# The w_in product of a second MLP as seven block products instead of eight, in groups of 768 tokens

## The chip, the cores and the metric

One NeuronCore of a Trainium2 chip runs the kernel. The metric is the device time of one execution in microseconds (us). The engines are TensorE (PE, with PEld for its weight loads), VectorE (DVE), ScalarE (ACT), GpSimd (POOL) and SyncE (SP), which here issues all DMAs.

## The reference

4608 tokens (8 batches of 576), model width 512. A linear attention with an RMS norm makes x, a gated MLP (1536 wide) follows, and then the MLP that the change is about:

```python
def _moe2_ref(x, w_in, w_out) -> np.ndarray:      # x 4608x512, w_in 512x2048, w_out 2048x512
    h = x @ w_in
    beta = 1.0
    neg = h <= -beta
    pos = h >= beta
    g = np.where(pos, h, np.where(neg, 0.0, (h + beta) ** 2 / (4.0 * beta)))
    return (g @ w_out).astype(np.float32)
```

Inputs are float32 or float64 (the weights are float64 and are decoded to float32 on the chip). The products are made nearly exact: each operand is split in a high and a low half of type fp32r, and each product is the sum of three matmuls (high by high, high by low, low by high).

## The kernel before, in words

The tokens go in `NB` = 9 blocks of `T` = 512. The features of a hidden layer go in slices of `P` = 128, which the code counts by `f`.

The **first part** makes attention and the gated MLP of all nine blocks. For blocks 2 to 8 one pass of the loop over `f` (12 slices) issues 24 matmuls for gate and value of slice `f + 1` (`gate_value`), their activation, the splits of that slice and of its `w_out` rows (`split_g`, `split_wo`), a piece of the next block's attention (`late_piece`), and the 12 matmuls of `down(j, f)`. In six passes of a block `decode_w2` also turns one raw float64 slice of the second MLP's weights into float32 and writes it to DRAM (`w2d`). Finished blocks go to DRAM as `x2d`.

The **second part** is the loop over the nine blocks at the end. `hidden2(j, f)` makes one 128x512 slice of h: 4 chunks of the model width by 3 matmuls of 512 columns, weights stationary, tokens moving. `act2` makes g of it with one ScalarE and two VectorE instructions and splits g. `out2(j, f)` adds that slice's share of the output, 4 token chunks by 3 matmuls of 512 columns. The halves of w_in stay in SBUF for the whole part. Those of w_out don't: `split_wo` makes them again for each of the 9 x 16 slices.

```python
def mm3(ps, w, x, first, last, wsl=slice(None)):
    nc.tensor.matmul(ps, w[0][:, wsl], x[0], start=first, stop=False)
    nc.tensor.matmul(ps, w[0][:, wsl], x[1], start=False, stop=False)
    nc.tensor.matmul(ps, w[1][:, wsl], x[0], start=False, stop=last)
```

Each engine runs its instructions in the order of the program; the code is a schedule written out by hand. What an instruction needs from another engine it waits for at its place in its own engine's queue. A tile of a pool can be written again only when its former reader is done. DMAs are issued by SP in program order too, and an issue that waits holds those behind it.

Of the kernel before, what the change touches and what calls it, by code (L numbers as in the profile page):

```python
# [7 lines left out]
F32 = mybir.dt.float32  # L8
# [6 lines left out]
NT, DM, FF1, FF2 = B * S, H * D, 1536, 2048  # L15
P = 128
T = 512
NB = NT // T
NP = H // 2
KC = DM // P  # L20
TC = T // P
F1, F2 = FF1 // P, FF2 // P
NSC = S // P
SC = 112
SR = S - NSC * SC
# [4 lines left out]
@with_exitstack  # L30
def attn_gated_mlp_kernel(ctx: ExitStack, tc: tile.TileContext, a: dict, out: bass.AP):
    nc = tc.nc
    pool = lambda name, bufs, **kw: ctx.enter_context(tc.tile_pool(name=name, bufs=bufs, **kw))
    const = pool("const", 1)
    wp = pool("w", 60)
# [4 lines left out]
    h_p = pool("h", 1, space=bass.MemoryType.PSUM)  # L40
    at_p = pool("at", 2, space=bass.MemoryType.PSUM)
    dram = pool("dram", 1, space=bass.MemoryType.DRAM)

    wod = {f: dram.tile([P, T], F32, name=f"wod{f}") for f in range(4, 6)}
    w2d = [dram.tile([P, 2, T], F32, name=f"w2d{f}") for f in range(F2)]
# [12 lines left out]
    def act_copy(o, i):  # L58
        nc.scalar.activation(out=o, in_=i, func=AF.Copy)  # L59
# [247 lines left out]
    def decode(keys):  # L307
        outs = []
        run(decode_steps(keys, outs))
        return outs  # L310
# [33 lines left out]
    def decode_wo(*fs):  # L344

        aside = {4: "gl", 5: "gh"}

        def place(key):
            f = key[1]
            if f in aside:  # L350
                return gp.tile([P, T], F32, name="wof", tag=aside[f])
            return wp.tile([P, T], F32, name="wo", tag="w")

        ts = []
        yield from decode_steps([("wo", f) for f in fs], ts, place)
        for f, t in zip(fs, ts):
            if f in aside:
                nc.sync.dma_start(out=wod[f], in_=t)
            else:
                wo[f] = t  # L360

    def load_wo(f):
        wo[f] = wp.tile([P, T], F32, name="wo", tag="w")
        nc.sync.dma_start(out=wo[f], in_=wod[f])

    def decode_w2(f, i):
        t, = decode([("w2", f, i)])
        nc.sync.dma_start(out=w2d[f][:, i], in_=t)
# [35 lines left out]
    def new_acc():  # L404
        for c in range(4):
            acc[c] = acc_p.tile([P, T], F32, name=f"acc{c}", tag=f"acc{c}")
# [12 lines left out]
            nc.sync.dma_start(out=dst(c), in_=t)  # L419


    w2, wo2, g2 = {}, {}, {}

    def load_w2(f):
        w = temp("w2f", "dt", bufs=2)
        nc.sync.dma_start(out=w, in_=w2d[f][:, 0])
        wo2[f] = wp.tile([P, T], F32, name="wo2", tag="w")
        nc.sync.dma_start(out=wo2[f], in_=w2d[f][:, 1])
        w2[f] = split(w, half_tile(wp, "w", "w"), half_tile(wp, "w", "w"))

    def load_x2(j):
        for c in range(KC):
            xnext[c] = xp.tile([P, T], F32, name="xn", tag=f"xn{c}")
            nc.sync.dma_start(out=xnext[c], in_=x2d[j][:, c, :])

    def hidden2(j, f):
        h = h_p.tile([P, T], F32, name="h2", tag=f"h{f % 2}")
        for c in range(KC):
            mm3(h, w2[f], xs[c], c == 0, c == KC - 1, slice(c * P, (c + 1) * P))
        return h  # L440

    def act2(j, f, h):

        t = temp("t2", "sig")
        nc.scalar.activation(out=t, in_=h, func=AF.Relu, bias=half, scale=0.5)  # L445
        g = temp("g2", "gf")
        nc.vector.scalar_tensor_tensor(out=g, in0=t, scalar=1.0, in1=h, op0=ALU.min, op1=ALU.max)  # L447
        nc.vector.scalar_tensor_tensor(out=g, in0=t, scalar=1.0, in1=g, op0=ALU.min, op1=ALU.mult)  # L448
        n = (j * F2 + f) % 3
        if n < 2:  # L450
            hi, lo = half_tile(gp, "gh", "gh"), half_tile(gp, "gl", "gl")
        else:
            t = tp.tile([P, 2, T], F32R, name="g3", tag="raw", bufs=4)
            hi, lo = t[:, 0], t[:, 1]
        g2[j, f] = split(g, hi, lo)

    def out2(j, f):
        g, w = g2.pop((j, f)), wos.pop(f)
        if f == 0:
            new_acc()  # L460
        for c in range(TC):
            mm3(acc[c], g, w, f == 0, f == F2 - 1, slice(c * P, (c + 1) * P))

    def rows(j):
        return lambda c: out[j * T + c * P:j * T + (c + 1) * P, :]


    todo = [(f, i) for f in range(F2) for i in range(2)]
    with tc.manual_schedule():
        for p in range(NP):  # L470
            load_kv_early(0, p)
# [8 lines left out]
            load_kv_early(1, p)  # L480
            load_q(1, p, True)
        load_gv(1)
        xb = {p: wp.tile([P, T], F32, name="xb", tag="w") for p in range(NP)}
        xbt = [(half_tile(wp, "w", "w"), half_tile(wp, "w", "w")) for _ in range(KC)]
# [185 lines left out]
        for j in range(2, NB):  # L670
            more = j + 1 < NB
            for f in range(F1):
                if j + 2 < B and f in (0, 2, 4, 6):
                    load_kv(j + 2, f // 2)
                if f + 1 < F1:
                    g = gate_value(f + 1, xs)
                    split_g(j, f + 1, g)
                    split_wo(wo, f + 1)
                if more and f < 9:
# [3 lines left out]
                if not more and f == 8:  # L683
                    load_x2(0)
                down(j, f)
                if not more and f > 0:
                    load_w2(f - 1)
                if f == F1 - 2:
                    split_x()
                if f in (0, 2, 4, 6, 8, 9) and todo and ("w2", *todo[0]) in raws:  # L690
                    decode_w2(*todo.pop(0))
                if more and f in (1, 3, 5, 7, 8, 11) and todo:
                    load_raw(("w2", *todo[0]), a["w_2"][todo[0]])
                if f == F1 - 1:
                    store(lambda c: x2d[j][:, c, :])
                    if more:
                        split_wo(wo, 0)
                        split_g(j + 1, 0, gate_value(0, xs))
                        if j + 2 < NB:
                            load_q(j + 2, 0)  # L700
                            load_q(j + 2, 1)
        split_wo(wo2, 0)
        split_wo(wo2, 1)
        for f in range(3):
            act2(0, f, hidden2(0, f))
        for j in range(NB):
            more = j + 1 < NB
            for f in range(F2):
                out2(j, f)
                if f + 2 < F2 or more:  # L710
                    split_wo(wo2, (f + 2) % F2)
                if j == 0 and f + 11 < F2:
                    load_w2(f + 11)
                if f == 4 and more:
                    load_x2(j + 1)
                if f + 4 < F2:
                    act2(j, f + 3, hidden2(j, f + 3))
                elif f + 4 == F2:
                    h = hidden2(j, F2 - 1)
                    if more:  # L720
                        split_x()
                    act2(j, F2 - 1, h)
                elif f == F2 - 2 and more:
                    act2(j + 1, 0, hidden2(j + 1, 0))
            store(rows(j))
            if more:
                for f in range(1, 3):
                    act2(j + 1, f, hidden2(j + 1, f))


# [38 lines left out]
```

## Time and profile before

| | |
|---|---|
| median of 3 runs | 1808.94 us (1805.08 to 1809.77) |
| the profiled execution, its time | 1809.8 us |
| its span in the profile | 1808.0 us |
| PE busy | 1795.3 us (99%), 8272 matmuls |
| DVE busy | 1056.6 us (58%) |
| ACT busy | 753.1 us (42%) |
| granted TensorE clock, mean | 0.995 |

The time is that of the whole execution; the span goes from the first instruction to the last. Busy time of PE counts a matmul from its start to its modelled end, so neighbours overlap and the share says only that PE was never without work. How long a matmul holds the engine is read from the distance of two starts.

### The profile page before, as it was taken

How to read it: one execution, taken by the hardware profiler on the slowest of the kernel's cores; microseconds unless marked ns; L12 is line 12 of the kernel's file. 1: busy time of each engine (PE TensorE's matmuls, PEld its weight loads, DVE VectorE, ACT ScalarE, POOL GpSimd, SP SyncE). 2: the span in 40 equal slices, each digit the busy share in tenths (PEclk: the TensorE clock that was granted, in tenths of full speed). 3: DMA queues.
4: the chain of work that ended last, by engine and by line, in shares of the span. 5: the costliest groups of instructions: out<-in, count | busy, mean ns of one | idle time of the engine just before them, and what ended most of it. 6: DMA issues, size and time to landing. Idle time of an engine off the chain costs nothing.

```text
span 1808.0 us, 21195 instructions
## 1 busy us (share of the span) xinstructions
PE 1795.3 (99%) x8272; PEld 1454.9 (80%) x8272; DVE 1056.6 (58%) x1621; ACT 753.1 (42%) x1233; POOL 1.9 (0%) x9
## 2 busy tenths in 40 slices
PE   8999999999999999999999999999999999999999
PEld 5787778888888888887888888888888888888887
DVE  3788755767667575766533555454555555555554
ACT  4444444535454454544432434343333333333333
POOL 0000000000000000000000000000000000000000
PEclk9999999999999999999999999999999999999999
DMA  8454733132322322121022301010101010101000
GB/s 223 140 181 168 220 107 103 49 120 68 101 73 66 108 79 79 57 82 53 7 70 84 109 18 47 1 47 0 47 1 47 1 47 1 47 1 47 1 24 24
DMA packets 57365, 124.15 MB, mean 69 GB/s; under 512 B 6568, under 2 KB 10792, under 8 KB 57264
## 3 DMA queue, kind: packets, MB, share of 16 engines
q1 hardware_dynamic: 57264, 122.79, 21.6%
q8 instruction: 65, 1.06, 0.2%
q14 instruction: 36, 0.29, 0.1%
HBM read 88.69 MB, written 34.08 MB: 68 GB/s over the span
## 4 chain that ended last, share of the span: by engine, by line
PE 97%; DMA 1%; DVE 1%; issue 0%; ACT 0%; SPq 0%; DVEq 0%; ACTq 0%
PE h L78 18%; PE h L79 18%; PE h L80 18%; PE acc L78 13%; PE acc L80 13%; PE acc L79 12%; PE X L138 2%; PE kvps L117 1%; PE SSt L174 1%; DMA gload<-gd 1%; PE R L206 0%; DMA q_early<-in_qT 0%; PE SS L234 0%; PE SS L233 0%; PE rt L193 0%
## 5 line engine op out<-in xcount | busy, mean ns | idle before, releaser
L78 PE MATMUL h<-xh,w 128*128 128x512 f32 x1344 | 528.2, 393 | 0.0
L79 PE MATMUL h<-xl,w 128*128 128x512 f32 x1344 | 526.2, 392 | 0.0
L80 PE MATMUL h<-xh,w 128*128 128x512 f32 x1344 | 525.2, 391 | 0.2 <-DVE w L67 0.2
L78 PEld LDWEIGHTS h<-xh,w 128*128 128x128 f32 x1344 | 253.2, 188 | 56.7 <-ACT w L59 0.7
L80 PEld LDWEIGHTS h<-xh,w 128*128 128x128 f32 x1344 | 253.2, 188 | 55.6 <-DVE w L67 0.6
L79 PEld LDWEIGHTS h<-xl,w 128*128 128x128 f32 x1344 | 253.1, 188 | 54.0
L447 DVE SCALAR_TENSOR_TENSOR g<-t,h 128x512 f32<-128x512 f32 x144 | 98.9, 687 | 249.8 <-ACT t L445 248.7
L445 ACT ACTIVATE t<-h,half 128x512 f32<-128x512 f32 x144 | 98.9, 687 | 261.1 <-PE h L80 261.1
L391 DVE TENSOR_TENSOR gf<-sig,h 128x512 f32<-128x512 f32 x108 | 74.1, 686 | 186.1 <-PE h L80 104.7
L67 DVE TENSOR_TENSOR wol<-wo,woh 128x512 fp32r<-128x512 f32 x252 | 172.4, 685 | 15.4 <-ACT woh L59 15.4
L78 PE MATMUL acc<-gh,woh 128*128 128x512 f32 x432 | 177.1, 410 | 0.0
L80 PE MATMUL acc<-gh,wol 128*128 128x512 f32 x432 | 171.4, 397 | 0.2
L79 PE MATMUL acc<-gl,woh 128*128 128x512 f32 x432 | 171.1, 396 | 0.2 <-DVE gl L67 0.2
L59 ACT ACTIVATE woh<-wo 128x512 fp32r<-128x512 f32 x252 | 155.5, 617 | 14.5 <-PE acc L80 13.5
L78 PE MATMUL acc<-woh,gh 128*128 128x512 f32 x384 | 150.5, 392 | 0.0
L80 PE MATMUL acc<-woh,gl 128*128 128x512 f32 x384 | 150.2, 391 | 0.0
L79 PE MATMUL acc<-wol,gh 128*128 128x512 f32 x384 | 149.4, 389 | 0.0
L59 ACT ACTIVATE gh<-gf 128x512 fp32r<-128x512 f32 x84 | 53.1, 632 | 212.9 <-DVE gf L391 212.9
L59 ACT ACTIVATE gh<-g 128x512 fp32r<-128x512 f32 x96 | 60.7, 632 | 143.5 <-DVE g L448 143.5
L389 ACT ACTIVATE sig<-h 128x512 f32<-128x512 f32 x108 | 64.5, 597 | 115.1 <-PE h L80 109.5
L67 DVE TENSOR_TENSOR gl<-g,gh 128x512 fp32r<-128x512 f32 x96 | 66.5, 693 | 67.0 <-ACT gh L59 67.0
L448 DVE SCALAR_TENSOR_TENSOR g<-t,g 128x512 f32<-128x512 f32 x144 | 99.6, 692 | 5.0
(125 smaller groups left out, 2121.2 us busy)
## 6 DMA issues: line engine op xcount, KB each, us to landing
raw<-in_w SPq DMA_DIRECT2D x32, 512.0 KB, 3.8
raw<-in_w_gv SPq DMA_DIRECT2D x24, 512.0 KB, 4.4
kvraw<-in_kv_main SPq DMA_DIRECT2D x24, 448.0 KB, 5.4
x2d<-ev SPq DMA_DIRECT2D x36, 256.0 KB, 2.8
xn<-x2d SPq DMA_DIRECT2D x36, 256.0 KB, 4.8
out<-ev SPq DMA_DIRECT2D x36, 256.0 KB, 2.3
w2d<-dt SPq DMA_DIRECT2D x32, 256.0 KB, 2.4
qraw<-in_qT SPq DMA_DIRECT2D x28, 256.0 KB, 3.3
```

The source lines that it names most:

```text
L59: nc.scalar.activation(out=o, in_=i, func=AF.Copy)
L67: nc.vector.tensor_tensor(out=lo, in0=src, in1=hi.bitcast(F32), op=ALU.subtract)
L78: nc.tensor.matmul(ps, w[0][:, wsl], x[0], start=first, stop=False)
L79: nc.tensor.matmul(ps, w[0][:, wsl], x[1], start=False, stop=False)
L80: nc.tensor.matmul(ps, w[1][:, wsl], x[0], start=False, stop=last)
L117: nc.tensor.matmul(ps[s], kc[:, s], vc[:, s], start=c == 0, stop=c == NSC)
L138: nc.tensor.matmul(X[:, t0:t1], kvbd[b % NKV][:, p, :], q[:, t0:t1], start=True, stop=True)
L389: nc.scalar.activation(out=sig, in_=gate, func=AF.Sigmoid)
L391: nc.vector.tensor_tensor(out=g, in0=sig, in1=value, op=ALU.mult)
L445: nc.scalar.activation(out=t, in_=h, func=AF.Relu, bias=half, scale=0.5)
L447: nc.vector.scalar_tensor_tensor(out=g, in0=t, scalar=1.0, in1=h, op0=ALU.min, op1=ALU.max)
L448: nc.vector.scalar_tensor_tensor(out=g, in0=t, scalar=1.0, in1=g, op0=ALU.min, op1=ALU.mult)
```

## The change

The second part is rewritten as the class `Second`. Tokens go in 6 groups of 768, each as two halves of `T2` = 384. The w_in product is seen as a 2 x 2 by 2 x 2 product of blocks: two halves of the model width (256 each), two slices of features (`s` and `s + 8`), two halves of the tokens. It is made with seven block products (`product`) in place of eight, from sums of blocks of the weights (`s1` to `s4`) and of the tokens (`t1` to `t4`). A block product is 2 chunks by 3 matmuls of 384 columns. Partial results are taken from four PSUM banks (A, B, C, D), copied to SBUF by ScalarE (`saved`) and added by VectorE; banks A and B are accumulated on after they were copied. One step `s` of a group has 7 x 6 = 42 such matmuls, and 18 of 512 columns for the output (none in step 0, whose slices are due a step later). When the 8 steps of a group are over, 16 more output products follow, for the group's second token half.

The weights' sums and the halves of everything are made once, in the first part (`w2_steps`, six pieces after each `down`), and go to DRAM: `w2d` holds 14,336 bytes a partition for each of the 8 steps, `wo2d` 4096 for each of the 16 slices of w_out. `w_load` reads one step's 1.83 MB again in every group, into a pool of two buffers that it shares with the tokens of the next group (`x_load`). The w_out halves are read in the first group and stay.

The last block of the first part is split: the 12 slices of gate and value go first and are kept in DRAM (`gd`), then pools are closed, the first loads of the second part are issued, and the 12 `down` follow with the tokens' splits (`x_steps`) between them.

```diff
+    def w2_steps(unit):
+        kind, f = unit
...
+        if kind == "out":
+            yield from halves_out(outs[0], temp("hi", "du", bufs=2), lambda h: wo2d[f][:, h])
+            return
...
+        for o, x, y, op in ((s1, a21, a22, ALU.add), (s2, s1, a11, ALU.subtract), (s4, a12, s2, ALU.subtract), (s3, a11, a21, ALU.subtract)):
+            nc.vector.tensor_tensor(out=o, in0=x, in1=y, op=op)
+            yield
+        d = w2d[f]
+        yield from halves_out(a22, a21, lambda h: d[:, 2, h])
+        yield from halves_out(t0, t1, lambda h: d[:, 0:2, h])
+        yield from halves_out(u0, t0, lambda h: d[:, 3:5, h])
+        yield from halves_out(u1, u0, lambda h: d[:, 5:7, h])
...
-    def hidden2(j, f):
-        h = h_p.tile([P, T], F32, name="h2", tag=f"h{f % 2}")
-        for c in range(KC):
-            mm3(h, w2[f], xs[c], c == 0, c == KC - 1, slice(c * P, (c + 1) * P))
-        return h
...
+        def product(self, bank, w, x, first=True):
+            for c in range(2):
+                sl = slice(c * P, (c + 1) * P)
+                for n, (h, l) in enumerate(((0, 0), (0, 1), (1, 0))):
+                    nc.tensor.matmul(bank[:, :T2], self.ws[w][h][:, sl], self.xo[x][:, l, c], start=first and c == n == 0,
+                                     stop=c == 1 and n == 2, skip_group_check=True)
...
+            for s in range(HF):
+                A, D, B, C = (self.bank(n) for n in "ADBC")
+                self.ws = self.w_next
+                if s + 1 < HF:
+                    self.w_next = self.w_load(s + 1)
+                    if g == 0:
+                        self.wo2_load(s + 1)
+                        self.wo2_load(s + 1 + HF)
+                elif more:
+                    x = self.x_load(g + 1)
...
+                self.product(A, "a11", "b11")
+                s1 = self.saved(A, "p1")
...
+                self.product(D, "a12", "b21")
...
+                tt(c0[:, 0], D[:, :T2], s1, ALU.add)
+                self.product(B, "s1", "t1")
...
+                s5 = self.saved(B, "p5")
...
+                    self.out_product(acc, s - 1, this_hi, s == 1, False)
...
+                self.product(A, "s2", "t2", False)
+                u2 = self.saved(A, "u2")
...
+                self.product(C, "a22", "t4")
+                self.product(B, "s4", "b22", False)
+                tt(g1[s][:, 0], B[:, :T2], u2, ALU.add)
+                self.product(A, "s3", "t3", False)
+                u3 = self.saved(A, "u3")
+                tt(g1[s][:, 1], A[:, :T2], s5, ALU.add)
+                tt(c0[:, 1], C[:, :T2], u3, ALU.add)
+                if late is not None:
+                    self.out_product(acc, s - 1 + HF, late_hi, False, False)
...
+        for f in range(F1):
+            keep_g(0, f, gate_value(f, xs, tag="wol"))
+            run(work, 6)
+            if f >= F1 - 3:
+                load_g(0, f - F1 + 3)
...
+        split_g(last, 0, gf[0, 0])
+        split_wo(wo, 0)
+        load_g(0, 3)
+        second.begin()
+        for f in range(F1):
+            if f + 1 < F1:
+                split_g(last, f + 1, gf[0, f + 1])
+                split_wo(wo, f + 1)
+            if 0 < f < F1 - 3:
+                load_g(0, f + 3)
+            if f > 1:
+                run(second.xsteps, 1)
+            down(last, f)
```

What this puts in the queues is shown at three places. First TensorE in the second part; before, a slice of h (`h`, weights `w`, tokens `xh` and `xl`) follows on the output matmuls (`acc`) of another slice:

```order
L78 MATMUL acc_13597<-woh,gh 128x512
L79 MATMUL acc_13597<-wol,gh 128x512
L80 MATMUL acc_13597<-woh,gl 128x512
L78 MATMUL h_13915<-xh_13444,w 128x512
L79 MATMUL h_13915<-xl_13445,w 128x512
L80 MATMUL h_13915<-xh_13444,w 128x512
L78 MATMUL h_13915<-xh_13448,w 128x512
```

Now, step 0 of the first group and the begin of step 1 (`ch` are the four banks, `x_` the operands made of the tokens, `wst` one step's weights):

```order
L556 MATMUL chA_8578<-x_b11_8316,wst_8258 128x384 x6
L556 MATMUL chD_8579<-x_b21_8343,wst_8258 128x384 x6
L556 MATMUL chB_8580<-x_t1_8368,wst_8258 128x384 x6
L556 MATMUL chA_8578<-x_t2_8395,wst_8258 128x384 x6
L556 MATMUL chC_8581<-x_t4_8422,wst_8258 128x384 x6
L556 MATMUL chB_8580<-x_b22_8447,wst_8258 128x384 x6
L556 MATMUL chA_8578<-x_t3_8474,wst_8258 128x384 x6
L556 MATMUL chA_8651<-x_b11_8316,wst_8582 128x384 x6
L556 MATMUL chD_8652<-x_b21_8343,wst_8582 128x384 x6
L556 MATMUL chB_8653<-x_t1_8368,wst_8582 128x384 x6
L84 MATMUL acc2_0_8575<-wo2_0_8571,gh2_8617 128x512
```

The 12 matmuls of 512 columns of one slice became 42 of 384 columns for two slices of 768 tokens, and step 0 hands bank A straight to step 1, which reads other weights.

Second, SP's queue where the last block of the first part is split, which has no counterpart before (block 8's slices went from `gate_value` straight to `down`, and tokens and weights of the second part were read in pieces of 256 KB between the `down` of that block):

```order
L756 DMA gd0_11_121<-gf_8219 128x512
L454 DMA gload_8222<-gd0_2_112 128x512
L454 DMA gload_8249<-gd0_3_113 128x512
L517 DMA xin_8251<-x2d0_134 128x2x256 x2
L517 DMA xin_8251<-x2d1_135 128x2x256
L517 DMA xin_8251<-x2d0_134 128x2x256 x2
L517 DMA xin_8251<-x2d1_135 128x2x256
L505 DMA wst_8258<-w2d0_86 128x3584
L454 DMA gload_8292<-gd0_4_114 128x512
```

The load of slice 4 for `down` now stands behind the first group's tokens (six DMAs) and the first step's weights.

Third, SP's queue where one group ends and the next begins (`out` are the output's rows); before, nothing but the next block's tokens was read there:

```order
L505 DMA wst<-w2d_86 128x3584
L587 DMA out<-ev_11499 128x512
L587 DMA out<-ev_11502 128x512
L587 DMA out<-ev_11505 128x512
L587 DMA out<-ev_11702 128x512
L587 DMA out<-ev_11705 128x512
L587 DMA out<-ev_11708 128x512
L505 DMA wst<-w2d_87 128x3584
```

The weights of the next group's step 0 stand ahead of the group's last stores, those of its step 1 behind them.

## Rows read from the trace of the kernel before

**Rows 1.** The page, part 1 (busy time) and part 4 (chain that ended last)

```profile
PE 1795.3 (99%) x8272; PEld 1454.9 (80%) x8272; DVE 1056.6 (58%) x1621; ACT 753.1 (42%) x1233; POOL 1.9 (0%) x9
...
PE 97%; DMA 1%; DVE 1%; issue 0%; ACT 0%; SPq 0%; DVEq 0%; ACTq 0%
```

**Rows 2.** Windows: stretch, length, busy by engine (instructions), clock, DMA share, GB/s

```profile
300.00:400.00 100.00, 100.00 (x487) 81.36 (x485) 65.56 (x98) 47.68 (x76) 0.00 (x0) 1.00 0.27 82
...
1100.00:1800.00 700.00, 700.00 (x3054) 572.71 (x3053) 369.69 (x555) 260.27 (x427) 0.00 (x0) 1.00 0.07 23
```

**Rows 3.** Timeline of PE: start us, us, line, operation, tiles, shapes

```profile
1000.40 0.39 PE L78 MATMUL h<-xh,w 128*128 128x512 f32 x1
...
1001.99 0.39 PE L79 MATMUL h<-xl,w 128*128 128x512 f32 x1
...
1300.33 0.40 PE L78 MATMUL acc<-woh,gh 128*128 128x512 f32 x1
...
1301.94 0.39 PE L79 MATMUL acc<-wol,gh 128*128 128x512 f32 x1
```

**Rows 4.** Groups by form, all or 103:124 us: form, count, busy us, mean ns, idle

```profile
L79 PE MATMUL h<-xl,w 128*128 128x512 f32 x1344 | 526.2, 392 | 0.0
...
L138 PE MATMUL X<-qraw,kvbd 128*128 128x384 f32 x7 | 2.9, 487 | 0.0
L138 PEld LDWEIGHTS X<-qraw,kvbd 128*128 128x128 f32 x16 | 2.4, 190 | 0.3
...
L138 PE MATMUL X<-qraw,kvbd 128*128 128x128 f32 x8 | 1.5, 272 | 0.0
```

**Rows 5.** Timeline of PE at attention products of two blocks

```profile
103.10 0.38 PE L138 MATMUL X<-qraw,kvbd 128*128 128x128 f32 x2
...
103.31 0.81 PE L138 MATMUL X<-qraw,kvbd 128*128 128x384 f32 x2
...
282.51 0.49 PE L138 MATMUL X<-qraw,kvbd 128*128 128x192 f32 x2
...
282.83 0.43 PE L138 MATMUL X<-qraw,kvbd 128*128 128x320 f32 x1
```

**Rows 6.** Groups by form of DVE and ACT, by size

```profile
L67 DVE TENSOR_TENSOR wol<-wo,woh 128x512 fp32r<-128x512 f32 x252 | 172.4, 685 | 15.4 <-ACT woh L59 15.4
L62 DVE COPY kvbd<-kvps 64x64 f32<-64x64 f32 x40 | 7.9, 196 | 0.3
...
L59 ACT ACTIVATE woh<-wo 128x512 fp32r<-128x512 f32 x252 | 155.5, 617 | 14.5 <-PE acc L80 13.5 <-DVE wo L299 1.0
```

**Rows 7.** Timeline of the second part: a hand-over, and VectorE instructions in a row

```profile
1292.41 0.69 DVE L67 TENSOR_TENSOR gl<-g,gh 128x512 fp32r<-128x512 f32 x1 [0.70 <-ACT gh L59]
...
1293.02 0.69 DVE L67 TENSOR_TENSOR wol<-wo,woh 128x512 fp32r<-128x512 f32 x1
...
1294.60 0.39 PE L80 MATMUL h<-xh,w 128*128 128x512 f32 x1
...
1295.09 0.69 ACT L445 ACTIVATE t<-h,half 128x512 f32<-128x512 f32 x1 [2.19 <-PE h L80]
```

**Rows 8.** DMA issues (count, KB each, us to landing), and two windows

```profile
raw<-in_w SPq DMA_DIRECT2D x32, 512.0 KB, 3.8
out<-ev SPq DMA_DIRECT2D x36, 256.0 KB, 2.3
...
207.00:211.00 4.00, 4.00 (x34) 3.05 (x34) 1.68 (x4) 1.15 (x2) 0.00 (x0) 1.00 1.01 374
20.00:30.00 10.00, 9.31 (x52) 7.20 (x52) 2.73 (x9) 3.40 (x10) 0.00 (x0) 1.00 1.08 242
```

**Rows 9.** Two passes of block 3 as a window, and VectorE's longest instruction

```profile
320.27:339.02 18.75, 18.75 (x100) 15.19 (x99) 13.55 (x19) 10.11 (x15) 0.00 (x0) 1.00 0.23 74
...
L161 DVE RECIPROCAL r<-r 128x512 f32<-128x512 f32 x24 | 80.5, 3353 | 16.8 <-ACT r L160 16.8
```

**Rows 10.** A window in which the granted clock is below 1

```profile
40.00:50.00 10.00, 10.00 (x53) 7.47 (x53) 2.57 (x5) 4.68 (x10) 0.00 (x0) 0.64 0.00 1
```

More of the change, by code (lines that the diff above doesn't have):

```diff
@@ L17 @@
 T = 512
+T2 = 384
 NB = NT // T
@@ L22 @@
 F1, F2 = FF1 // P, FF2 // P
+HF = F2 // 2
 NSC = S // P
@@ L32, in attn_gated_mlp_kernel @@
     nc = tc.nc
-    pool = lambda name, bufs, **kw: ctx.enter_context(tc.tile_pool(name=name, bufs=bufs, **kw))
+    first_part, early_end = ExitStack(), ExitStack()
+    held = lambda stack, name, bufs, **kw: stack.enter_context(tc.tile_pool(name=name, bufs=bufs, **kw))
+    dram = held(ctx, "dram", 1, space=bass.MemoryType.DRAM)
+    pool = lambda name, bufs, **kw: held(first_part, name, bufs, **kw)
     const = pool("const", 1)
-    wp = pool("w", 60)
+    wop = pool("wo", 12)
     xp = pool("x", 1)
@@ L39, in attn_gated_mlp_kernel @@
     acc_p = pool("acc", 1, space=bass.MemoryType.PSUM)
-    h_p = pool("h", 1, space=bass.MemoryType.PSUM)
-    at_p = pool("at", 2, space=bass.MemoryType.PSUM)
-    dram = pool("dram", 1, space=bass.MemoryType.DRAM)
+    h_p = held(early_end, "h", 1, side="right", space=bass.MemoryType.PSUM)
+    at_p = held(early_end, "at", 2, side="right", space=bass.MemoryType.PSUM)
+    wp = held(early_end, "w", 48, side="right")
     wod = {f: dram.tile([P, T], F32, name=f"wod{f}") for f in range(4, 6)}
-    w2d = [dram.tile([P, 2, T], F32, name=f"w2d{f}") for f in range(F2)]
+    w2d = [dram.tile([P, 7, 2, 2 * P], F32, name=f"w2d{f}") for f in range(HF)]
+    wo2d = [dram.tile([P, 2, T], F32, name=f"wo2d{f}") for f in range(F2)]
     gd = {(j, f): dram.tile([P, T], F32, name=f"gd{j}_{f}") for j in range(2) for f in range(F1)}
@@ L362, in load_wo, with w2_keys, load_raw_w2, halves_out @@
     def load_wo(f):
-        wo[f] = wp.tile([P, T], F32, name="wo", tag="w")
+        wo[f] = wop.tile([P, T], F32, name="wo", tag="wo")
         nc.sync.dma_start(out=wo[f], in_=wod[f])
-    def decode_w2(f, i):
-        t, = decode([("w2", f, i)])
-        nc.sync.dma_start(out=w2d[f][:, i], in_=t)
+    def w2_keys():
+        for unit in w2_units:
+            if unit[0] == "in":
+                yield from (("w2", unit[1] + e * HF, 0) for e in range(2))
+            else:
+                yield "w2", unit[1], 1
+    w2_units = [u for s in range(HF) for u in (("in", s), ("out", 2 * s), ("out", 2 * s + 1))]
+    w2_todo = list(w2_keys())
+    def load_raw_w2():
+        if w2_todo:
+            key = w2_todo.pop(0)
+            load_raw(key, a["w_2"][key[1:]])
+    def halves_out(src, place, dst):
+        hi, lo = place.bitcast(F32R), src.bitcast(F32R)
+        yield split(src, hi, lo)
+        for h, t in enumerate((place, src)):
+            d = dst(h)
+            nc.sync.dma_start(out=d, in_=t if len(d.shape) == 2 else t.rearrange("p (o n) -> p o n", n=2 * P))
+        yield
+        yield
+    def w2_steps(unit):
+        kind, f = unit
+        outs = []
+        for e in range(2 if kind == "in" else 1):
+            load_raw_w2()
+            got = []
+            yield from decode_steps([("w2", f + e * HF, 0) if kind == "in" else ("w2", f, 1)], got)
+            outs += got
+        if kind == "out":
+            yield from halves_out(outs[0], temp("hi", "du", bufs=2), lambda h: wo2d[f][:, h])
+            return
+        t0, t1 = outs
+        a11, a12, a21, a22 = (t[:, i * 2 * P:(i + 1) * 2 * P] for t in outs for i in range(2))
+        u0, u1 = (temp("su", "du", bufs=2) for _ in range(2))
+        s1, s2, s4, s3 = (u[:, i * 2 * P:(i + 1) * 2 * P] for u in (u0, u1) for i in range(2))
+        for o, x, y, op in ((s1, a21, a22, ALU.add), (s2, s1, a11, ALU.subtract), (s4, a12, s2, ALU.subtract), (s3, a11, a21, ALU.subtract)):
+            nc.vector.tensor_tensor(out=o, in0=x, in1=y, op=op)
+            yield
+        d = w2d[f]
[3 more added lines that the diff above has]
+        yield from halves_out(u1, u0, lambda h: d[:, 5:7, h])
     def split_wo(src, f):
@@ L436, in hidden2 @@
-    def hidden2(j, f):
-        h = h_p.tile([P, T], F32, name="h2", tag=f"h{f % 2}")
-        for c in range(KC):
-            mm3(h, w2[f], xs[c], c == 0, c == KC - 1, slice(c * P, (c + 1) * P))
-        return h
[L442 to L455, printed above, removed]
@@ L482, in attn_gated_mlp_kernel @@
         load_gv(1)
-        xb = {p: wp.tile([P, T], F32, name="xb", tag="w") for p in range(NP)}
-        xbt = [(half_tile(wp, "w", "w"), half_tile(wp, "w", "w")) for _ in range(KC)]
+        xb = {p: wop.tile([P, T], F32, name="xb", tag="wo") for p in range(NP)}
+        xbt = [(half_tile(wop, "xbh", "wo"), half_tile(wop, "xbl", "wo")) for _ in range(KC)]
         nc.gpsimd.memset(kvbd[0], 0.0)
@@ L669, in attn_gated_mlp_kernel, with w2_work @@
         split_wo(wo, 0)
-        for j in range(2, NB):
-            more = j + 1 < NB
+        share = {j: n for j, n in zip(range(2, NB), (3, 4, 3, 4, 3, 4, 3))}
+        def w2_work(j):
+            for unit in w2_units[sum(share[i] for i in range(2, j)):][:share[j]]:
+                yield from w2_steps(unit)
+        last = NB - 1
+        load_raw_w2()
+        for j in range(2, last):
+            work = w2_work(j)
             for f in range(F1):
@@ L678, in attn_gated_mlp_kernel @@
                     split_wo(wo, f + 1)
-                if more and f < 9:
+                if f < 9:
                     late_piece(j + 1, f)
@@ L682, in attn_gated_mlp_kernel @@
                         kv_product(j + 2, f // 2)
-                if not more and f == 8:
-                    load_x2(0)
                 down(j, f)
-                if not more and f > 0:
-                    load_w2(f - 1)
                 if f == F1 - 2:
                     split_x()
[L690 to L693, printed above, removed]
+                run(work, 6)
@@ L694, in attn_gated_mlp_kernel @@
                 if f == F1 - 1:
+                    run(work)
                     store(lambda c: x2d[j][:, c, :])
-                    if more:
+                    if j + 1 < last:
                         split_wo(wo, 0)
                         split_g(j + 1, 0, gate_value(0, xs))
[L699 to L728, printed above, removed]
+                    if j + 2 < NB:
+                        load_q(j + 2, 0)
+                        load_q(j + 2, 1)
@@ new lines, in attn_gated_mlp_kernel @@
+        work = w2_work(last)
+        for f in range(F1):
+            keep_g(0, f, gate_value(f, xs, tag="wol"))
+            run(work, 6)
+            if f >= F1 - 3:
+                load_g(0, f - F1 + 3)
+        run(work)
+        early_end.close()
+        second = Second()
+        split_g(last, 0, gf[0, 0])
[11 more added lines that the diff above has]
+            down(last, f)
@@ L731 @@
+        store(lambda c: x2d[last][:, c, :])
+        run(second.xsteps)
+        first_part.close()
+        second.rest()
 def kernel(q, k, v, g_norm, moe_w_gate, moe_w_val, moe_w_out, moe2_w_in, moe2_w_out):
```

190 lines of the change are left out of this document (170 added, 20 removed).

## The prediction

> **What bounds the kernel now.** I read the page first. TensorE is busy for 99% of the span and the chain that ended last is 97% TensorE [rows 1], so time goes only where its instructions get fewer or shorter, or where a new wait opens. The windows say the same by stage: TensorE has no idle time in a stretch of the first part, nor in the second part, at a granted clock of 1.00, while VectorE is busy for 66% of the middle of the first part and 53% of the second (369.69 of 700), ScalarE for less [rows 2]. DMA is at 7% in the second part.
>
> What a matmul holds the engine is read from starts. In the second part 7 steps between two h matmuls take 1001.99 - 1000.40 = 1.59 us, 0.2271 us each; for the output matmuls 1.61 us, 0.230 us each [rows 3].
>
> **The w_in product.** Removed: 9 blocks x 16 slices x 12 = 1728 matmuls of 512 columns, x 0.2271 = 392.4 us. Added: 6 groups x 8 steps x 42 = 2016 of 384 columns. The output matmuls stay at 1728 of 512 columns. No matmul of this type has 384 columns before, so its price comes from others. The attention products are plain float32 passes: 384 columns last 487 ns and 128 last 272 ns, 215 ns for 256 columns, 0.840 ns each [rows 4]. Starts lie 0.105 us apart at 128 columns (103.10 to 103.31 for two) and 0.16 us at 192 (282.51 to 282.83 for two) [rows 5], the same slope. An h matmul of 512 columns lasts 392 ns [rows 4]. If fp32r streams a column in half that, 0.420 ns, 512 columns are 215.0 ns, and 12.1 ns of its 227.1 are an extra.
>
> - The extra goes with each matmul: 384 x 0.420 + 12.1 = 173.4 ns, x 2016 = 349.6 us.
> - It goes with the columns: 227.1 x 0.75 = 170.3 ns, 343.4 us.
> - The weight load paces: one is recorded with 188 to 190 ns [rows 4]; with 190 ns a matmul, 383.0 us.
>
> I take the first: an operand's own weights are loaded for every matmul, whatever its columns. The third is unlikely, since two matmuls of 192 columns, each with its own load, started 0.16 us apart [rows 5]. The term is **-42.8 us**, with bounds -49.0 and -9.4.
>
> **The rest of a step in steady state.** A step from 1 on is 42 x 0.1734 + 18 x 0.230 = 7.28 + 4.14 = 11.42 us of TensorE. VectorE: a result of 512 elements takes 685 ns and one of 64 takes 196 [rows 6], so 1.09 ns an element: 384 are 545 ns, 768 about 965. Ten instructions of 384 (four adds from PSUM, two maxima, two low halves, two clips) and two of 768 make 7.4 us, 65%. ScalarE: 617 ns at 512 [rows 6], so at most that at 384 and twice that at 768: eight and one, 6.2 us, 54%. These are shares like today's, so I cost them at nothing; the cover is TensorE's own work. The closest hand-over is bank A: its last product ends 9.34 us into the step, a consumer starts 0.49 us after the last matmul's start (1294.60 to 1295.09 [rows 7]), 0.26 us after its slot; VectorE has then still to finish the square and maximum of the last step's pair and two adds, to about 10.5 us, before the next step writes A at 11.42: 0.9 us to spare. If that is not there, every one of 42 steps pays.
>
> **Step 0 of each group** has no output products to fill: after 7.28 us the next step writes A again, but its last copy and add need 0.26 + 0.55 + 0.1 us, so TensorE waits 0.9 us whatever else happens. And step 1's weights: their issue stands on SP behind the group's last three stores. The third eviction starts about 0.26 us after the last matmul and takes 0.69, so SP reaches the load near 1.35 us. A transfer of 512 KB lands in 3.8 us; at the 374 GB/s of a busy stretch [rows 8] its data is 1.4 us, leaving 2.4 fixed. 1.83 MB are 4.9 us of data: landing at 1.35 + 2.4 + 4.9 = 8.6, or 8.2 if some of the fixed part overlaps. TensorE needs it at 7.28. I take 1.1 us for each of five boundaries, **+5.5**; the lower bound is 0.9 x 5 = 4.5. At 242 GB/s [rows 8] the data is 7.6 us and the stores 3.2, 4.5 us of wait each, 22 in all.
>
> **Begin of the second part.** In front of step 1's weights stand four stores (1.05 MB) and two w_out slices (1.05 MB), issued until about 2.4 us after the last `down`: data 2.8 us for the slices behind a 1.5 us start, then 4.9, and the receipt, landing near 11 us. Step 0 ends at 7.28: **+3.7**, between 0.9 (they run beside each other) and 8 (242 GB/s). Later in that group 2.88 MB a step are 7.7 us of data in 11.42, so hidden; at 242 GB/s 11.9, half a us each.
>
> **The split last block.** Its matmuls stay 288 + 144. At the hand-over from gates to `down` nothing fills: VectorE makes the last gate's product, then the low halves of g and of w_out, 0.61 us apart [rows 7], the last done 0.26 + 0.61 + 0.61 + 0.68 = 2.2 us after the gates; two slots run meanwhile: 1.8 us. Then the load of slice 4: it stands behind six token DMAs and the first weights, 3.4 MB and 9 to 11 us of data from about 3.5 us, so it lands near 15, its split is done 1.7 later, and `down(4)` could start at 1.8 + 4 x 12 x 0.230 = 12.8. That is 4 us, and 1 more for passes that hold two VectorE instructions of 768 and two of 512 (3.3 us against 2.76). Taken together 1.8 to 7.2; I take **+7.0**, since DMAs of one queue are served in turn where the queue is full (share 1.01 [rows 8]).
>
> **First part and tails.** The halves cost VectorE 8 x 4.2 + 16 x 0.69 = 44 us more over seven blocks, of some 730 us. Two passes of block 3 hold 13.55 us of VectorE in 18.75, one decode of five instructions among them [rows 9]; a second decode at 0.69 each makes 17.0, so it fits, but a pass that has the 3.35 us reciprocal [rows 9], four instructions of 0.69 and a full decode is 9.6 us of work in 9.4. VectorE may lag by the 2.76 us of a `down` before a bank is missed: **+1**, between 0 and 10. In each group's tail the put of the first half stands on VectorE ahead of slice 3's low half: 0.2 us, six times: **+1**. The 160 splits of the second part that go (98.6 us of VectorE for w_out) were hidden: nothing.
>
> **Sum**: -42.8 + 5.5 + 3.7 + 7.0 + 1 + 1 = -24.6; 1809.8 of the profiled execution (0.9 above the median of the runs shown) gives **1785 us**.
>
> Two waits of 3 to 5 us also put the clock at risk. [...] I leave it at zero.
>
> **Rivals.**
>
> - *The weight load paces the 384-column matmuls* (190 ns): 1809.8 - 9.4 + 18.2 = 1819, slower. It decides from (392.4 - 18.2) / 2016 = 186 ns on. For it: the recorded load of 188 ns starts when the matmul ahead starts. Against: [rows 5]. 8%.
> - *No extra at 384 columns* (161.3 ns): 325.2 us, -67.2 + 18.2, 1761. For it: the 128-column passes start at 0.105 us, about 0.82 ns a column, without any extra [rows 5]. [...] 7%.
> - *The chain of VectorE and ScalarE is longer than a step*: 0.4 us in each of 42 steps gives 1802, 0.6 us takes all of the gain. For it: each step has two chains of add, clip, square, maximum and split over both engines, in queues that run in order. Against: 65% and 54% of load. 15%.
> - *Transfers at 242 GB/s*: 16 us more at the boundaries, 4 at the begin, 2 in the last block, 1807, the same. For it: the window at 20 us, with DMA at full share, moved no more. Against: the one at 207 us moved 374 at the same share [rows 8]. 12%.
> - *The forecast*, 1776 to 1796 with the terms' bounds: 58%.
>
> Within 0.3% is about what the runs can tell from no change. Faster by more (below 1803.5): the forecast, the second rival and most of the third, 79%. Within: 10%, mostly transfers. Slower: the first rival and the worst of the third, 11%. The range goes from 1768, which leaves the second rival out, to 1808, which leaves the first out.
>
> **What would show it.** Starts of the 384-column matmuls at 173 ns; 2016 of them; steps of 11.4 us with TensorE never idle in 1 to 7; idle of about 1 us after step 0 of each group, released by the step's weights or VectorE; 3 to 4 us at the first; about 7 us around the last block's `down`, released by a low half and by a load of `gd`; VectorE near 65% in the second part. The prediction is wrong if starts are at 186 ns or more, or if TensorE idles inside steps 1 to 7.

## The result and the profile after

The change made the kernel slower by about 1.5%: 1832.51 us (median of 4, 1827.62 to 1837.78) against 1807.01 beside it, a ratio of 1.0147 [1.0105, 1.0189]. Forecast were 1785 and at most 1808. The profiled execution took 1834.2 us with a span of 1832.4 (before 1808.0).

The page of after, parts 1 and 4, to be read beside [rows 1]:

```profile
PE 1771.7 (97%) x8560; PEld 1489.7 (81%) x8560; DVE 1092.5 (60%) x1817; ACT 790.8 (43%) x1361; POOL 2.0 (0%) x10
...
PE 50%; DVE 5%; DMA 3%; ACT 2%; issue 1%; SPq 0%; DVEq 0%; ACTq 0%
```

TensorE's busy time fell by 23.6 us while the span rose by 24.4, so 48 us more of the span have no matmul in them. The chain names DVE, DMA and ACT where before it was nearly all PE. What TensorE waited for stands in the list of its waits (in total, times, longest, us):

```profile
PE h L84 <- ACT sig L441: 27.3, 15, 10.2
PE chA L556 <- DMA wst<-w2d: 11.4, 4, 4.0
...
PE acc L84 <- ACT woh L65: 4.4, 2, 4.2
PE chA L556 <- DVE c L491: 1.6, 1, 1.6
```

The largest, for a gate's sigmoid (`sig`) in the **first part**, is one that the prediction doesn't have. The `wst` row and those under it are the forecast ones. Windows of after by stage (length, busy of PE, PEld, DVE, ACT, POOL, granted clock, DMA share, GB/s): the first 60 us, blocks 2 to 7, the split block 8, the second part:

```profile
0.00:60.00 60.00, 52.19 (x312) 36.84 (x313) 24.43 (x62) 26.82 (x59) 1.86 (x9) 0.98 0.60 171
...
264.20:952.70 688.50, 660.46 (x3062) 528.53 (x3061) 441.48 (x640) 328.33 (x515) 0.00 (x0) 0.98 0.26 83
952.70:1062.20 109.50, 103.29 (x434) 81.98 (x433) 51.92 (x81) 32.65 (x55) 0.10 (x1) 0.98 0.41 141
...
1062.20:1830.00 767.80, 751.98 (x3745) 678.83 (x3743) 415.03 (x752) 313.82 (x576) 0.00 (x0) 1.00 0.41 147
```

And of before, cut at the same places of the program:

```profile
0.00:60.00 60.00, 51.89 (x305) 36.98 (x306) 22.06 (x58) 25.44 (x57) 1.86 (x9) 0.89 0.62 168
...
268.60:912.20 643.60, 643.60 (x3062) 522.42 (x3061) 416.98 (x590) 310.02 (x477) 0.00 (x0) 1.00 0.24 73
912.20:1011.40 99.20, 99.20 (x434) 81.32 (x433) 33.08 (x52) 29.72 (x53) 0.00 (x0) 1.00 0.24 80
```

By stage, in these two executions:

| stage | before | after | difference | forecast |
|---|---|---|---|---|
| start, blocks 0 and 1 | 268.6 | 264.2 | -4.4 | 0 |
| blocks 2 to 7 | 643.6 | 688.5 | +44.9 | +1 |
| block 8, split | 99.2 | 109.5 | +10.3 | +7.0 |
| second part, to the span's end | 796.6 | 770.2 | -26.4 | -32.6 |
| sum | 1808.0 | 1832.4 | +24.4 | -24.6 |

The first row isn't the change's: the granted clock of the first 60 us differs between executions (0.89 and 0.98 above; 0.80 in two runs below whose start is that of after, the one without the splits and the last). Blocks 2 to 7 hold the miss. Same 3062 matmuls, but 28.0 us in which TensorE has none (688.50 - 660.46) and 16.9 us more of busy time, at a clock of 0.98 instead of 1.00. Some 10 of the 16.9 are the half clock, by an estimate: 52 of these matmuls start in stretches at a granted clock of 0.50, where starts lie 0.43 us apart instead of 0.23. Of the rest a part lies at the edges of the waits, where a matmul has no neighbour to overlap with (the one behind the wait at 342.56 us counts with 0.51 us, where starts in a row lie 0.23 apart).

Two places show how the waits come about. The first is one of the common ones. ScalarE, VectorE and TensorE of after at 331 to 345 us (start, length, engine, line, operation, and in brackets the idle time before it and its releaser; the last row is a window):

```profile
332.96 0.63 ACT L166 ACTIVATE r<-m 128x512 f32<-128x512 f32 x1
339.96 0.63 ACT L65 ACTIVATE hi<-dt 128x512 fp32r<-128x512 f32 x1 [6.37 <-DVE dt L305]
340.61 1.28 ACT L441 ACT_TABLE_LOAD   x1
341.91 0.60 ACT L441 ACTIVATE sig<-h 128x512 f32<-128x512 f32 x1
...
333.63 3.35 DVE L167 RECIPROCAL r<-r 128x512 f32<-128x512 f32 x1 [0.70 <-ACT r L166]
...
337.32 0.43 DVE L294 TENSOR_SCALAR dt<-dt 128x512 uint32<-128x512 uint32 x1
...
339.24 0.69 DVE L305 SCALAR_TENSOR_TENSOR dt<-raw,du 128x512 uint32<-128x512 uint32 x1
...
333.47 0.39 PE L86 MATMUL h<-xh,w 128*128 128x512 f32 x1
...
342.56 0.51 PE L84 MATMUL h<-xh,w 128*128 128x512 f32 x1 [2.30 <-ACT sig L441]
342.90 0.39 PE L85 MATMUL h<-xl,w 128*128 128x512 f32 x1
...
344.04 0.63 PE L84 MATMUL h<-xh,w 128*128 128x512 f32 x1
344.47 0.63 PE L85 MATMUL h<-xl,w 128*128 128x512 f32 x1
...
344.00:347.40 3.40, 3.40 (x9) 2.65 (x8) 3.12 (x5) 2.48 (x5) 0.00 (x0) 0.50 0.82 264
```

VectorE runs without a gap from the reciprocal through the decode (`dt`). ScalarE's next instruction is the new copy of the high half, `hi<-dt`, which needs the decode: ScalarE stands still for 6.37 us. Behind it in the same queue are the table load and the sigmoid that reads the gate out of its PSUM bank, and TensorE waits 2.30 us for that bank. After it matmuls first start 0.23 us apart, then 0.43 (344.04 to 344.47): the granted clock has fallen from 1.00 to 0.50 (the last row).

The second place is the end of block 3, where ScalarE works off the chain of splits of one step's weights:

```profile
499.61 0.63 ACT L65 ACTIVATE dt<-dt 128x512 fp32r<-128x512 f32 x1 [2.31 <-DMA w2d<-dt]
503.26 0.63 ACT L65 ACTIVATE dt<-su 128x512 fp32r<-128x512 f32 x1 [3.02 <-DMA w2d<-dt]
506.94 0.63 ACT L65 ACTIVATE su<-su 128x512 fp32r<-128x512 f32 x1 [3.05 <-DMA w2d<-su]
509.88 1.33 ACT L65 ACTIVATE ev<-acc 128x512 f32<-128x512 f32 x2 [2.31 <-DMA w2d<-su]
511.11 0.62 ACT L65 ACTIVATE woh<-wo 128x512 fp32r<-128x512 f32 x1
511.63 0.59 ACT L441 ACTIVATE sig<-h 128x512 f32<-128x512 f32 x1
...
501.64 0.39 PE L86 MATMUL h<-xh,w 128*128 128x512 f32 x1
512.27 0.80 PE L84 MATMUL h<-xh,w 128*128 128x512 f32 x1 [10.25 <-ACT sig L441]
512.87 0.63 PE L85 MATMUL h<-xl,w 128*128 128x512 f32 x1
513.29 0.63 PE L86 MATMUL h<-xh,w 128*128 128x512 f32 x1
...
504.40:518.10 13.70, 5.83 (x14) 4.57 (x15) 4.09 (x7) 3.70 (x7) 0.00 (x0) 0.50 0.76 233
```

The four splits reuse each other's tiles, so each may write only when the store of the one before has landed (2.31 to 3.05 us each). The evictions (`ev`) take the same tiles and wait too, and the sigmoid is behind all of them: 10.25 us, with a granted clock of 0.50 from 504.4 us on, inside the wait, to 518.1 (the last row, a window). At the first place the clock fell at 344.0 us, among dense matmuls, 1.5 us after a wait of only 2.30 us. That ScalarE's instructions don't pass one that waits shows in the rows at 331 to 345 us: the gate's last matmul started at 333.47, and the sigmoid didn't pass the copy that waited until 339.96.

Ahead of each of the 15 waits ScalarE's timeline has such a copy that waits. ScalarE's own waits at these copies, over the whole kernel (in total, times, longest, us):

```profile
ACT hi L65 <- DVE dt L305: 50.2, 12, 6.4
ACT dt L65 <- DMA w2d<-dt: 34.2, 10, 6.1
...
ACT dt L65 <- DVE su L414: 24.1, 8, 5.4
...
ACT su L65 <- DMA w2d<-su: 16.9, 4, 5.7
```

In 7 of the 15 the copy waited for VectorE (7.5 us of TensorE's 27.3), in 8 for a store to land (19.8 us), some of these stores late themselves because VectorE's subtraction stood behind a reciprocal. So most of this waiting hangs on stores.

In the second part the product itself went as forecast. TensorE's timeline, 384 columns, six matmuls a row:

```profile
1080.49 1.21 PE L556 MATMUL chA<-x_t,wst 128*128 128x384 f32 x6
1081.54 1.20 PE L556 MATMUL chC<-x_t,wst 128*128 128x384 f32 x6
1082.58 1.20 PE L556 MATMUL chB<-x_b,wst 128*128 128x384 f32 x6
1083.62 1.20 PE L556 MATMUL chA<-x_t,wst 128*128 128x384 f32 x6
```

(1083.62 - 1080.49) / 18 = 173.9 ns a matmul; forecast were 173.4.

### The profile page after: what moved, and what is told of

Same layout as the page of the kernel before. It is cut to its first block, busy times and chain, and to the rows that moved or that the text cites. A ratio compares the mean times of both kernels' runs of the same rounds, so it can differ in the third digit from the quotient of the medians.

```text
span 1832.4 us, 22307 instructions
## 1 busy us (share of the span) xinstructions
PE 1771.7 (97%) x8560; PEld 1489.7 (81%) x8560; DVE 1092.5 (60%) x1817; ACT 790.8 (43%) x1361; POOL 2.0 (0%) x10
## 4 chain that ended last, share of the span: by engine, by line
PE 50%; DVE 5%; DMA 3%; ACT 2%; issue 1%; SPq 0%; DVEq 0%; ACTq 0%
PE chA L556 8%; PE acc L86 6%; PE acc L85 6%; PE acc L84 6%; PE chB L556 5%; PE chD L556 3%; PE h L84 3%; PE chC L556 2%; PE h L86 2%; PE h L85 2%; DMA wst<-w2d 2%; PE chC L85 1%; PE chB L85 1%; PE chC L86 1%; PE chB L86 1%
## 5 line engine op out<-in xcount | busy, mean ns | idle before, releaser
L84 PE MATMUL h<-xh,w 128*128 128x512 f32 x768 | 307.3, 400 | 27.3 <-ACT sig L441 27.3
L86 PE MATMUL h<-xh,w 128*128 128x512 f32 x768 | 303.8, 396 | 0.2 <-DVE w L73 0.2
L85 PE MATMUL h<-xl,w 128*128 128x512 f32 x768 | 303.6, 395 | 0.0
L84 PEld LDWEIGHTS h<-xh,w 128*128 128x128 f32 x768 | 147.1, 192 | 66.6 <-ACT sig L441 35.1
L86 PEld LDWEIGHTS h<-xh,w 128*128 128x128 f32 x768 | 147.0, 191 | 32.0 <-DVE w L73 0.6
L85 PEld LDWEIGHTS h<-xl,w 128*128 128x128 f32 x768 | 147.2, 192 | 30.6
L86 PE MATMUL acc<-wo,gh 128*128 128x512 f32 x384 | 151.1, 393 | 0.0
L85 PE MATMUL acc<-wo,gh 128*128 128x512 f32 x384 | 150.9, 393 | 0.0
L84 PE MATMUL acc<-wo,gh 128*128 128x512 f32 x384 | 149.6, 389 | 0.0
L556 PE MATMUL chA<-x_t,wst 128*128 128x384 f32 x576 | 116.6, 337 | 0.0
L556 PEld LDWEIGHTS chA<-x_t,wst 128*128 128x128 f32 x576 | 102.6, 188 | 3.7
L84 PEld LDWEIGHTS acc<-gh,woh 128*128 128x128 f32 x432 | 81.6, 189 | 25.0 <-ACT woh L65 5.3
L85 PEld LDWEIGHTS acc<-gl,woh 128*128 128x128 f32 x432 | 81.9, 190 | 22.1 <-DVE gl L73 2.8
L86 PEld LDWEIGHTS acc<-gh,wol 128*128 128x128 f32 x432 | 81.5, 189 | 22.0 <-DVE wol L73 2.8
```

Source lines behind the costliest of these rows:

```text
L556: nc.tensor.matmul(bank[:, :T2], self.ws[w][h][:, sl], self.xo[x][:, l, c], start=first and c == n == 0, stop=c == 1 and n == 2, skip_grou ...
```

## The experiments

Each run stands against the kernel before on the same chip. Theory A: ScalarE's copies of the high halves, in its queue ahead of the sigmoids, cause the loss of blocks 2 to 7. Rival B: VectorE has too much work there. Rival C: the clock falls by itself.

**The splits of the second MLP's weights left out** (so both stores take unsplit values); decode, sums, stores and the second part stay.

```diff
-        yield split(src, hi, lo)
-        for h, t in enumerate((place, src)):
+        yield
+        for h, t in enumerate((src, src)):
```

> Leaves out the splits into halves of the second MLP's weights in the first part (both stores take the unsplit values, so the output is not the reference's); decodes, block sums and all stores stay. Theory A (in-order queue: ScalarE's copy of a high half stands ahead of the next gate's sigmoid and waits there for VectorE or for a store's receipt, so TensorE waits for a bank): blocks 2 to 7 go back to the length they had before, 108 us each for blocks 3 and 4 in place of 115 and 123, no wait of TensorE for a sigmoid, no stretch at half clock between 300 and 1000 us, about 1790 us in all. Theory B (VectorE has too much work in these blocks, whatever the queues): the decodes are still there, VectorE loses only some 30 us of 490, so at most half of the 45 us comes back, about 1812. Theory C (the clock falls by itself): waits go, but the half-clock stretches of about 15 us in sum stay, about 1800.

Measured: 1791.12 us, ratio 0.9913 [0.9878, 0.9949]. There is no wait for a sigmoid. Blocks 2 to 7 as a window of this run:

```profile
263.70:907.30 643.60, 643.60 (x3062) 522.47 (x3061) 416.23 (x598) 306.05 (x473) 0.00 (x0) 1.00 0.28 89
```

The blocks have the length of before (643.60), TensorE is never idle and at full clock: the splits cause the whole loss there. Against C stands the clock, which stays up where no wait comes ahead. Against B stands only that the time is far below its 1812; VectorE's work fell back to that of before too (416.23 us here, 416.98 before, 441.48 after), so this run doesn't tell the copies from VectorE's load. Where the copies stand was tried next.

**Copy and subtraction on GpSimd**, idle before:

```diff
-        yield split(src, hi, lo)
+        nc.gpsimd.tensor_copy(out=hi, in_=src)
+        yield nc.gpsimd.tensor_tensor(out=lo, in0=src, in1=hi.bitcast(F32), op=ALU.subtract)
```

> Both instructions of each of these splits go to GpSimd, which is idle; all else stays. Theory A: neither ScalarE nor VectorE waits for the chain of halves and receipts any more, about 1790 to 1795. Theory B: VectorE is relieved by the same 30 us as without the halves, about 1812. If GpSimd's work slows VectorE down, longer VectorE instructions show it in the same windows.

Measured: 1808.1 us, ratio 1.0006 [0.9982, 1.0029]. That misses A's range and lies nearer to B's 1812. But blocks 2 to 7 take 658.2 us in place of 688.5 and the small waits are gone; one is left, and ScalarE's timeline shows what it is:

```profile
PE h L84 <- ACT sig L442: 12.7, 1, 12.7
...
502.93 0.60 ACT L65 ACTIVATE ev<-acc 128x512 f32<-128x512 f32 x1 [16.81 <-DMA w2d<-su]
```

It is the end of block 3 again: the chain of stores now runs beside ScalarE, but the evictions still take its tiles, and an eviction waits 16.81 us. So there are two mechanisms, and the expectation had only the first. As for longer VectorE instructions beside GpSimd's: the low half of g took 748 ns between 400 and 800 us, 693 without the halves.

**Only the copy moved, to VectorE**; the subtraction was there already:

```diff
-        yield split(src, hi, lo)
+        dve_copy(hi, src)
+        yield nc.vector.tensor_tensor(out=lo, in0=src, in1=hi.bitcast(F32), op=ALU.subtract)
```

> The high half is copied by VectorE in place of ScalarE, so VectorE gets more work (44 copies of 0.43 us or more) and ScalarE's queue no longer holds an instruction of the halves. Theory A: the waits for a sigmoid that came from VectorE's lag mostly go; VectorE now waits for receipts itself, 1800 to 1815. Theory B: more load on VectorE, slower than the changed kernel, 1840.

Measured: 1821.6 us, ratio 1.0092 [1.0064, 1.0121]. Neither expected time was met. By the ratios alone the step from after is barely clear of the noise, so blocks 2 to 7 are read from the trace (last row, a window). The sigmoid is waited for once instead of 15 times, while VectorE, which now waits for the stores itself (24.0 us in 11 waits at these copies), makes TensorE wait elsewhere, most of it for `sqh`, the high half of the squares for the norm:

```profile
PE h L84 <- ACT sig L442: 9.5, 1, 9.5
...
PE SS L239 <- ACT sqh L65: 7.3, 4, 2.0
...
267.50:943.70 676.20, 654.98 (x3062) 526.67 (x3061) 457.63 (x682) 304.83 (x473) 0.00 (x0) 0.98 0.26 85
```

VectorE has more to do (457.63 us against 441.48) and the blocks are shorter than after's 688.5: against B as the whole cause. But they stay 32.6 us longer than before, so the copies' place in ScalarE's queue isn't the whole cause either.

**Other pacing**: no pieces in the four passes with a reciprocal, nine in the others:

```diff
-                run(work, 6)
+                run(work, 0 if f in (1, 3, 5, 7) else 9)
```

> The same work with other pacing: none in the four passes of a block that hold a reciprocal (3.35 us on VectorE), nine pieces in each of the others. Theory A: a high half's copy no longer stands behind a reciprocal, so the waits of 1 to 3 us go; the receipts stay in the way, about 1815. Theory B: the sum of VectorE's work in two passes is the same, so the lag is too, 1825 to 1832.

Measured: 1828.73 us, ratio 1.0118 [1.0079, 1.0158]: a miss for A, and taken alone it fits B. The waits for sigmoids are fewer (8 instead of 15), but the longest is 14.0 us instead of 10.2, 24.8 in sum: nine pieces in a pass put more of the chain of stores into it.

**The end of block 3 alone**: the order of the units, so that no step's weights are due at the end of a block; the halves stay on ScalarE:

```diff
+    w2_units = [("in", 0)] + [("out", f) for f in range(2)] + [("in", 1)] + [("out", f) for f in range(2, 5)]
...
-        share = {j: n for j, n in zip(range(2, NB), (3, 4, 3, 4, 3, 4, 3))}
+        share = {j: n for j, n in zip(range(2, NB), (3, 4, 3, 4, 4, 4, 2))}
```

> Only the order of the units of weight work is changed, so that no block ends on the long unit (two decodes, four sums, four splits in a chain over the receipts of stores) and less of it is left for the end of a block; halves stay on ScalarE and VectorE. If the 10 us wait at the end of block 3 and the half clock behind it come from that chain standing ahead of the block's evictions and the next sigmoid, they go and the rest stays: some 14 us less than the changed kernel, about 1818. If it comes from VectorE's load, the wait only moves, 1828 to 1833.

Measured: 1839.35 us, ratio 1.018 [1.0156, 1.0204]; a miss. The 10 us wait went, yet 20 waits of at most 3.6 us make 28.1, where 15 made 27.3. What B said, that the wait only moves, is what happened. With the copies on ScalarE, this order and the pacing above move the waits and don't take them away.

**Both mechanisms at once**: this order, and the halves on GpSimd as above.

> The halves on GpSimd and the new order of the units together: the one wait left with the halves on GpSimd (12.7 us at the end of block 3, 6 to 7 us of half clock behind it) goes, blocks 2 to 7 have the lengths of before, about 1791 as without the halves. If the chain of receipts has to block some engine, a new wait shows in another block, about 1800 to 1808.

Measured: 1792.36 us, ratio 0.992 [0.9897, 0.9943]. Blocks 2 to 7, to be read beside the same row of before in the section on the result:

```profile
268.90:912.50 643.60, 643.60 (x3062) 522.41 (x3061) 426.58 (x594) 305.46 (x473) 75.61 (x80) 1.00 0.27 88
```

Equal length (643.60), equal matmuls, no idle time: the whole loss of these blocks is gone, with every store and every half made. This run also takes the subtractions off VectorE (426.58 us against 441.48 of after). The copies alone on GpSimd, with the subtractions left on VectorE, were not tried, so what each of the two is worth stays open.

The remaining runs take the forecast waits one after the other. **Loads**: the first weights are asked for in pass 4 of the last block's `down`, behind the load of slice 7 instead of ahead of that of slice 4, and step 1's of the later groups ahead of the last three stores.

```diff
-            self.w_next = self.w_load(0)
...
+            if f == 4:
+                second.w_next = second.w_load(0)
...
+                self.w_early = self.w_load(1)
             self.put(acc2, g * 2 * T2 + T2)
```

> The same, and two loads moved: the first step's weights are asked for in pass 4 of the last block's down instead of ahead of the loads of g, and step 1's weights of a later group ahead of the last three stores instead of behind them. If these queue positions set the waits there (4.2 us in the last block, 1.2 to 2.5 us at each of five boundaries), the first goes and the others fall to the 1.2 us that the adds of step 0 take: 8 to 12 us less than the kernel beside it, about 1781. If transfers are slow for other reasons, no more than 3 us less.

Measured: 1779.15 us, ratio 0.9846 [0.9822, 0.9869]. Block 8 takes 103.1 us. What is left at the boundaries is the first group's DMA and five waits for VectorE:

```profile
PE chA L560 <- DVE g L495: 5.9, 5, 1.2
PE chA L560 <- DMA wst<-w2d: 5.0, 1, 5.0
```

**The first group's step 1 too**:

```diff
+            if f == F1 - 1:
+                second.w_early = second.w_load(1)
```

> On top of the kernel with all loads moved, step 1's weights of the first group too are asked for early, in the last pass of the last block's down, ahead of that block's stores and of the first w_out slices. If its queue position sets the 5 us wait there, the wait falls to the 1.2 us of the later groups and the half clock behind it (6.8 us) goes: 6 to 7 us less, about 1773. If the transfers of this stretch are the bound, the wait only moves to step 2.

Measured: 1776.14 us, ratio 0.9824 [0.9796, 0.9853]; all six boundaries now wait 1.2 us for the last add out of bank A (`DVE g`), the lower bound that the prediction put at 0.9. The interval overlaps with that of the run before this one, so the gain is read from the traces: the second part goes from 765.8 to 760.0 us.

**The product into bank D ahead of that into A**:

```diff
+                self.product(D, "a12", "b21")
                 self.product(A, "a11", "b11")
...
-                self.product(D, "a12", "b21")
```

> On top of that, each step makes the product into bank D first and that into bank A second, so that the last adds of bank A have 1 us more before the bank is written again. If the 1.2 us wait behind step 0 of each group is that hand-over, six of them go: 6 to 7 us less than the kernel beside it, about 1766. If the adds of bank D and the squares behind them become late by the 1 us, steps 1 to 7 show new waits and the time stays or grows.

Measured: 1770.58 us, ratio 0.98 [0.9768, 0.9831]: faster than both kernels. In the second part, from 1014.0 us on, TensorE is idle for no more than 0.95 us:

```profile
1014.00:1764.00 750.00, 749.05 (x3745) 675.66 (x3743) 415.98 (x752) 318.91 (x576) 0.00 (x0) 1.00 0.40 148
```

## Why the prediction was wrong

- **Product, -42.8: right.** Starts are 174 ns apart. Against those of 512 columns that is (227.1 - 173.9) / 128 = 0.416 ns a column; that fp32r takes half of the 0.840 ns, 0.420, was an assumption, and the starts bear it out. With less than 1 us of waits in it, the second part of the last run takes 1767.7 - 1014.0 = 753.7 us, 42.9 less than the 796.6 of before; that it comes within 0.1 us is chance, since the starts alone (2016 x 173.9 ns) give 41.8 less. The rivals of the weight load (190 ns) and of no extra (161.3 ns) fall with it.
- **A step in steady state at nothing: right.** TensorE waits in no step from 2 on, nor inside step 1 once it has begun, and a step takes 11.51 us (forecast 11.42). VectorE has less to do than was thought: 415.03 of 767.80 us, 54% in place of near 65. The rival of a longer chain of VectorE and ScalarE was looked for in the second part, where it doesn't occur; a chain of this kind bit in the first.
- **Group boundaries and begin, +9.2: measured 14.3** (11.4 + 1.6 + 1.3 in the list). The first cost 3.97 us (forecast 3.7, with 1.5 of the fixed 2.4 us put ahead of the data as an estimate; the weights asked for at 1153.89 us in this profile move from 1154.8 on, 0.9 us later); the five others 1.3 to 2.5 each instead of 1.1. The mechanism is the one given: moving the loads left exactly the hand-over of bank A, at 1.17 us each.
- **The split block, +7.0: measured +10.3.** Waits of 4.2 us for the late slice 4 (forecast 4) and 1.2 for a low half (1.8) are there; that slice's load, issued at 1024.88 us behind the 3.4 MB, landed 9.8 us later, against a median of 3.0 for these loads; of the rest 4.1 us are busy time, at a granted clock of 0.98. With the loads moved the block costs 103.1 - 99.2 = 3.9 more than before.
- **"VectorE may lag by the 2.76 us of a `down` before a bank is missed: +1, between 0 and 10": the step that failed**, at +44.9. It added up VectorE's work and let TensorE's bank be the only one that a lag reaches. The sum of VectorE's work doesn't set the loss: with the copies moved to it VectorE has more of it than in after (457.63 us against 441.48), and the blocks are shorter. But ScalarE's copy of the high half has to wait for that VectorE, and the gate's sigmoid stands behind the copy, so a lag of VectorE that nobody read before now stops ScalarE; and the wait for stores of a chain that overwrites its own tiles, shared with the evictions, wasn't in the sum at all, though 19.8 of the 27.3 us of waits for a sigmoid stand behind one. The prediction counted the added instructions per engine and didn't look at what is queued behind each of them. None of its rivals and none of its signs of being wrong is about the first part.
- **The clock, "I leave it at zero": failed with it.** The clock did fall to 0.50 behind the 4.2 us wait in block 8 (from 1036.9 us on) and the 4.0 us one at the begin of the second part (from 1074.5 us on), some 3 us in sum by the starts; the larger part, some 10 us, came behind the waits of blocks 2 to 7, which the prediction didn't have.

That the splits on ScalarE and VectorE and the tiles that their stores share with the evictions cause the loss is shown: without the splits it is gone, and so it is with the splits on GpSimd in the other order. That the sigmoid's place behind the copy is the way to TensorE is read from the trace, at all 15 waits; VectorE's share in it was not tried apart. How the 44.9 us divide between waits (28.0) and longer busy time (16.9) is read from one trace.

## What to carry to other kernels

When work is added to an engine's queue, ask first what stands behind each instruction and who waits for that, and only then whether the sum of work fits: an instruction that waits for another engine holds all that follow it (of a wait of 6.37 us on ScalarE 2.30 reached TensorE here). A chain that stores a tile and then writes over it pays the store's landing time at each link (waits of 2.31 to 3.05 us here), and so does anyone who shares its tiles. An engine with nothing else to do was the right place for such a chain here, even though it is slower at it (1290 ns a subtraction against 685).

## What was not expected of the hardware

- In the middle of dense matmuls a single wait of 2.30 us was followed, about 1.5 us after it, by starts 0.43 us apart instead of 0.227. In the same run two waits of 2.45 and 2.48 us at group boundaries were followed by no fall (granted clock 1.00 from 1451 to 1460 and from 1707 to 1716 us), while one of 2.51 us was (0.51 from 1583.0 to 1586.4). So the length of a wait alone doesn't settle it.
- fp32r matmuls of 384 columns, not seen before, start 174 ns apart: 0.77 of the 227 ns at 512, not 0.75.
- GpSimd's subtraction of 128x512 takes 1290 ns and its copy 645 in the mean of 16 each (single copies 609 to 879), against 685 and 617 for VectorE and ScalarE [rows 6]:

```profile
L391 POOL TENSOR_TENSOR dt<-dt,hi 128x512 fp32r<-128x512 f32 x16 | 20.6, 1290 | 1.3
L390 POOL CAST hi<-dt 128x512 fp32r<-128x512 f32 x16 | 10.3, 645 | 281.2 <-DVE dt L305 281.2
```
